# A delta-rule attention with two feed-forward layers on one core: the first block's state, Gram products and weight casts in another order

## The chip, the cores and the metric

One NeuronCore of a Trainium2 chip. The metric is the device time of one execution in microseconds (us); the number given for a kernel is the median of its runs.

## What is computed

Delta-rule attention over 32 heads (4 batches of 8) of 768 tokens and width 48: a state of 48 x 48 per head is read by the query and corrected by the key, token by token. Its output, 3072 tokens of width 384, goes through two feed-forward layers with hidden width 2048: the first with ELU, the second with h times sigmoid(1.702 h).

```python
for t in range(S):
    y[:, :, t] = einsum('bhd,bhde->bhe', q[:, :, t], state)
    v_old = einsum('bhde,bhd->bhe', state, kt)
    state = state + bt * einsum('bhd,bhe->bhde', kt, vt - v_old)
x = elu(x @ w_in) @ w_out          # layer 0
x = swish(x @ w_in2) @ w_out2      # layer 1
```

## The kernel before, in words

**Attention.** The tokens are cut into 12 chunks (c) of 64, two chunks to a pass (p, 0 to 5). In a chunk the token recurrence becomes a triangular system. Its parts are functions of `chunk`, `gram`, `inverse`, `join16` and `across`:

- `gram`: the products of the keys with themselves (L203), into the two-bank PSUM tile `wide` (there is one), copied to `z` by ScalarE in one whole copy (L190) and two for the far halves (`self.rest`, L193);
- `inverse`: for both chunks of a pass, rows of a 16 x 16 or 32 x 32 inverse on VectorE, two operations a row (L317, L322), then a scaling and a transpose (L330, L336). Passes 0 to 2 (`FINE`) have 16 x 16 blocks that `join16` (TensorE L395, L410) joins; `across` and, in pass 0, `t2`, `m1`, `m2` (L442, L457) give the off-diagonal part;
- `nv` scales v (VectorE, L490); `kq` is k times q (L504), `mask` masks it on VectorE (L515);
- `ks` is k times the state (L562), taken from v by VectorE (L567); `w` applies the inverse (L579, copies L585 to L588); `state` is the state's new part (L602), which VectorE adds to the old one (L609) or, for chunk 0, VectorE and ScalarE copy;
- `ya`, `yb`: the output (L629, L645), copied and split into high and low parts by ScalarE and VectorE (L655, L656).

`ks`, `kq`, `w`, `state`, the output and `m2` all use `wide` once the units run, so each waits until the one before it has been read.

**Units.** A unit is one block of 128 hidden columns (m, 0 to 15) for one pass's 512 tokens: 16 units for a pass, 6 passes, 2 layers, 192 units. Its nine up products (L748, high and low parts in fp32r) give `h`; ScalarE makes Relu and Exp (L757, L758), VectorE the second ELU step (L761), ScalarE the rounded hidden block `gh` (L770), VectorE the rest `gl` (L773). The nine down products (L785) come two units later (`LAG`) and sum in the three banks `acc0` to `acc2`; unit 2 is the first that does.

**Weights.** Layer 0's 16 weight blocks arrive as 64-bit words and are converted in pass 0's units by `prep`: `rebase` (ScalarE, L707), `shift` (VectorE, L714), `rest` (VectorE, L717, merges the words) with `high` (ScalarE, L724, the rounded part), and `low` (GpSimd, L728, the difference). Unit t does the shift, merge and cast of block t+2, the difference of block t+1, the rebase of block t+4, and the load of block t+6, which a one-element copy on ScalarE (L702) holds back. SP issues all loads, in program order.

**Order.** Everything is in one order written out by hand, and each engine takes its part of it in that order. First comes a straight list: both chunks of pass 0 up to their outputs, with the first weights and 11 steps of pass 1's inverse in between (`run(...)`, `also(n)`). Unit 0's up products start at 63.83 us. Then each unit emits: up products, first ELU step, `fill`, `gl` of the unit before, `mid`, second ELU step, down products of two units before, `end`, `gh`, `tail`. Attention of the passes to come is put at slots: slot s is the middle (even) or the end (odd) of unit s // 2. The steps of the inverses are spread over the `fill` of a range of units by `spread`, by costs in a table (`COST`, `slack`). Slots at issue here: Gram 4 at 0 and Gram 5 at 2, with their two extra copies in the tail of the same unit and the fill of the next; chunk 1's `state` at 4.

## Time and profile before

| | |
|---|---|
| median of 3 runs | 991.79 us (989.93 to 992.45) |
| profiled execution | 990.37 us |
| its span, first to last instruction | 988.6 us |
| TensorE busy | 941.7 us (95%) |
| VectorE, ScalarE, GpSimd busy | 594.4, 464.2, 83.1 us |
| mean granted TensorE clock | 0.984 of full |

In the rows PE is TensorE's matmuls and PEld its weight loads, DVE VectorE, ACT ScalarE, POOL GpSimd, SP the engine that issues the loads. A row names an operation as line, output tile <- input tiles. "idle before <- releaser" is the time that the engine stood idle ahead of it and whose end let it go; "issue" means that the profile shows nothing that it waited for. PEclk is the clock that TensorE was granted, as a share of 2.4 GHz. A busy TensorE at half clock does half the work.

### The profile page before, as it was taken

How to read it: one execution, taken by the hardware profiler on the slowest of the kernel's cores; microseconds unless marked ns; L12 is line 12 of the kernel's file. 1: busy time of each engine (PE TensorE's matmuls, PEld its weight loads, DVE VectorE, ACT ScalarE, POOL GpSimd, SP SyncE). 2: the span in 40 equal slices, each digit the busy share in tenths (PEclk: the TensorE clock that was granted, in tenths of full speed). 3: DMA queues.
4: the chain of work that ended last, by engine and by line, in shares of the span. 5: the costliest groups of instructions: out<-in, count | busy, mean ns of one | idle time of the engine just before them, and what ended most of it. 6: DMA issues, size and time to landing. Idle time of an engine off the chain costs nothing.

```text
span 988.6 us, 25639 instructions
## 1 busy us (share of the span) xinstructions
PE 941.7 (95%) x11520; PEld 773.2 (78%) x11520; DVE 594.4 (60%) x1048; ACT 464.2 (47%) x753; POOL 83.1 (8%) x72
## 2 busy tenths in 40 slices
PE   4866899999999999999999999999999999999998
PEld 4755677778878887888887888888888888888886
DVE  6886887677987877886445676733333333333332
ACT  6636475644374465444446675533333233333332
POOL 3021252010010001000000100101001001010000
PEclk9977999999999999999999999999999999999999
DMA  7263342303211230210114801010010010100000
GB/s 240 88 208 104 108 154 91 114 4 92 83 56 58 74 98 19 92 44 34 34 49 157 371 1 64 1 54 11 1 65 1 1 64 1 64 1 1 33 1 32
DMA packets 20174, 68.33 MB, mean 69 GB/s; under 512 B 3168, under 2 KB 4704, under 8 KB 20064
## 3 DMA queue, kind: packets, MB, share of 16 engines
q1 hardware_dynamic: 19920, 66.56, 20.0%
q8 instruction: 90, 1.47, 0.6%
q14 instruction: 20, 0.16, 0.1%
q10 hardware_dynamic: 144, 0.13, 0.0%
HBM read 57.25 MB, written 9.44 MB: 67 GB/s over the span
## 4 chain that ended last, share of the span: by engine, by line
PE 85%; DVE 8%; ACT 4%; issue 2%; DMA 0%; POOL 0%; ACTq 0%; DVEq 0%; POOLq 0%
PE h L748 38%; PE acc L785 27%; PE accn L785 10%; PE ps_w L562 1%; PE ps_w L504 1%; PE ps_w L579 1%; PE ps_w L602 1%; PE ps_w L629 1%; PE ps_w L203 1%; DVE tmp L317 1%; PE ps_w L645 1%; ACT z L193 1%; DVE t L761 1%; DVE W L322 1%; DVE x L515 1%
## 5 line engine op out<-in xcount | busy, mean ns | idle before, releaser
L748 PE MATMUL h<-xh,wt 128*128 128x512 f32 x1152 | 396.4, 398 | 0.0
L785 PE MATMUL acc<-gh,wt 128*128 128x512 f32 x864 | 292.6, 393 | 0.5 <-DVE xo L846 0.5
L748 PEld LDWEIGHTS h<-xh,wt 128*128 128x128 f32 x1152 | 218.5, 190 | 48.1 <-DVE xl L656 0.2
L748 PE MATMUL h<-xl,wt 128*128 128x512 f32 x576 | 226.6, 393 | 0.0
L773 DVE TENSOR_TENSOR gl<-t,gh 128x512 fp32r<-128x512 f32 x192 | 138.7, 722 | 93.8 <-ACT gh L770 93.6
L785 PEld LDWEIGHTS acc<-gh,wt 128*128 128x128 f32 x864 | 162.7, 188 | 35.7 <-issue 0.9
L770 ACT CAST gh<-t 128x512 fp32r<-128x512 f32 x192 | 119.3, 621 | 118.8 <-DVE t L761 62.2
L785 PE MATMUL acc<-gl,wt 128*128 128x512 f32 x432 | 168.7, 390 | 0.0
L767 DVE TENSOR_TENSOR t<-t,h 128x512 f32<-128x512 f32 x96 | 66.0, 687 | 168.9 <-ACT t L764 168.9
L764 ACT ACTIVATE t<-h 128x512 f32<-128x512 f32 x96 | 57.3, 597 | 187.2 <-PE h L748 187.2
L748 PEld LDWEIGHTS h<-xl,wt 128*128 128x128 f32 x576 | 109.5, 190 | 21.1
L757 ACT ACTIVATE t<-h 128x512 f32<-128x512 f32 x96 | 57.4, 598 | 100.3 <-PE h L748 99.8
L785 PE MATMUL accn<-gh,wt 128*128 128x512 f32 x288 | 96.4, 389 | 0.0
L761 DVE SCALAR_TENSOR_TENSOR t<-t,h 128x512 f32<-128x512 f32 x96 | 65.6, 684 | 51.0 <-ACT t L758 50.5
L785 PEld LDWEIGHTS acc<-gl,wt 128*128 128x128 f32 x432 | 81.4, 188 | 16.1
L785 PEld LDWEIGHTS accn<-gh,wt 128*128 128x128 f32 x288 | 54.1, 188 | 11.3
L758 ACT ACTIVATE t<-t 128x512 f32<-128x512 f32 x96 | 60.7, 632 | 3.1
L812 POOL TENSOR_TENSOR xl<-x1r,xh 128x512 fp32r<-128x512 f32 x18 | 24.1, 1339 | 407.4 <-ACT xh L811 314.4
L785 PE MATMUL accn<-gl,wt 128*128 128x512 f32 x144 | 56.0, 389 | 0.0
L728 POOL TENSOR_TENSOR wt<-w,wt 128x768 fp32r<-128x768 f32 x16 | 31.5, 1974 | 70.7 <-ACT wt L724 70.7
L515 DVE TENSOR_TENSOR x<-ps_w,mask_p 64x512 f32<-64x512 f32 x44 | 30.2, 687 | 11.2 <-PE ps_w L504 10.7
L717 DVE SCALAR_TENSOR_TENSOR w<-raw,w 128x768 uint32<-128x768 uint32 x32 | 35.2, 1101 | 0.9
(190 smaller groups left out, 832.6 us busy)
## 6 DMA issues: line engine op xcount, KB each, us to landing
raw<-in_w SPq DMA_DIRECT2D x32, 768.0 KB, 7.6
kt<-in_kT SPq DMA_DIRECT2D x12, 512.0 KB, 4.5
x<-in_qT SPq DMA_DIRECT2D x24, 256.0 KB, 4.2
kg<-in_kT SPq DMA_DIRECT2D x9, 512.0 KB, 4.8
kn<-in_kn SPq DMA_DIRECT2D x12, 384.0 KB, 3.5
x1d<-xo SPq DMA_DIRECT2D x12, 384.0 KB, 2.9
x1r<-x1d SPq DMA_DIRECT2D x6, 768.0 KB, 4.7
vn<-in_vn SPq DMA_DIRECT2D x11, 384.0 KB, 3.4
```

The lines of the kernel that those rows point to most:

```text
L515: v.tensor_tensor(out=g["x"][k][self.tok(k), 8 * hf:8 * hf + 8], in0=i, in1=self.mask_p[t].unsqueeze(1).to_broadcast(list(i.shape)), op=AL ...
L717: v.scalar_tensor_tensor(out=bits[m], in0=words(m, 0), scalar=29, in1=bits[m], op0=ALU.logical_shift_right, op1=ALU.bitwise_or)
L728: (v if layer else nc.gpsimd).tensor_tensor(out=wt[:, 1], in0=bits.pop(m).bitcast(F32), in1=wt[:, 0].bitcast(F32), op=ALU.subtract)
L748: nc.tensor.matmul(hps, wt[:, part, k * P:(k + 1) * P], src[:, k], start=(i == 0), stop=(i == 3 * NK - 1))
L757: nc.scalar.activation(out=t, in_=hps, func=AF.Relu, scale=-1.0)
L758: nc.scalar.activation(out=t, in_=t, func=AF.Exp, scale=-1.0)
L761: nc.vector.scalar_tensor_tensor(out=t, in0=t, scalar=-1.0, in1=hps, op0=ALU.add, op1=ALU.max)
L764: nc.scalar.activation(out=t, in_=hps, func=AF.Sigmoid, scale=1.702)
L767: nc.vector.tensor_tensor(out=t, in0=t, in1=hps, op=ALU.mult)
L770: nc.scalar.copy(gh, t)
L773: nc.vector.tensor_tensor(out=gl, in0=t, in1=gh.bitcast(F32), op=ALU.subtract)
L785: self.nc.tensor.matmul(self.acc[c], wt[:, part, DM + c * P:DM + (c + 1) * P], src, start=(m == 0 and i == 0), stop=(m == NM - 1 and i == 2),)
```

## The change

In the straight list: chunk 1's `nv` comes first, the first cast behind the rebase of block 2, the first difference ahead of chunk 0's output, and norm and scale of pass 1's inverse ahead of chunk 1's `w` (13 steps of that inverse instead of 11 before unit 0). Chunk 1's `state` goes to slot 0 and into `acc0`, `acc1`. Gram 4 and 5 go to slots 2 and 4, each with all three copies right behind it. In layer 0 the cast `high` leaves `rest` and stands first in the unit's `tail`, behind `gh`. Loads of chunk 2's k and chunk 3's v move by a unit, chunk 3's parts by half a unit to a unit and a half. Later passes: `m2` ahead of `ks`, and the last pass half a unit later. `spread` carries negative room over to the next unit.

```diff
--- before.py
+++ after.py
@@ -590,7 +590,7 @@
         def state():
             if last:
                 return
-            if first:
+            if c < 2:
                 ps = self.banks(0)
             else:
                 both = self.wide()
@@ -730,11 +730,12 @@
         ms = list(ms)
         steps = []
         for j, m in enumerate(ms):
-            t = [lambda m=m: shift(m), lambda m=m: (rest(m), high(m))]
+            t = [lambda m=m: shift(m), (lambda m=m: (rest(m), high(m))) if layer else (lambda m=m: rest(m))]
             if j:
                 t.append(lambda m=ms[j - 1]: low(m))
             steps += t
         steps.append(lambda: low(ms[-1]))
+        self.highs = [lambda m=m: high(m) for m in ms]
         return [lambda gate=False, m=m: load(m, gate) for m in ms], [lambda m=m: rebase(m) for m in ms], steps
 
     def up(self, wt, x, act_fn):
@@ -883,7 +884,11 @@
             sizes = sizes or [1.0] * len(fns)
             left = [max(0.2, 1.0 - taken.get(u, 0.0)) for u in range(u0, u1)]
             if u0 in slack:
-                left = [max(0.2, slack.get(u, 0.0) + (2.8 if u > NM - 3 else 1.2)) for u in range(u0, u1)]
+                left, over = [], 0.0
+                for u in range(u0, u1):
+                    over += slack.get(u, 0.0) + (2.8 if u > NM - 3 else 1.2)
+                    left.append(max(0.2, over))
+                    over -= left[-1]
             part, u, room = sum(left) / sum(sizes), u0, left[0]
             for f, size in zip(fns, sizes):
                 while room <= 0.0 and u + 1 < u1:
@@ -916,6 +921,7 @@
             return t.rearrange("p (u t) -> p u t", u=32)
 
         loads, bases, conv = self.prep(0, range(NM), lambda m: (self.wp, "wt"))
+        highs = self.highs
         join = {c: self.later(lambda c=c: self.join16(c, home), 6) for c in range(6)}
         part = {0: (0,), 1: (1, 2), 2: (3,), 3: (4, 5)}
         steps = self.later(lambda: self.inverse(0, lambda: turned(0)), len(self.sizes(0)))
@@ -983,17 +989,18 @@
         run(j1[4], j1[5], c1["t2"])
         also(2)
         run(bases[0], c0["m1"], c1["m1"], c0["nv"], c1["mask"], c0["m2"], bases[1], c1["m2"])
-        run(conv[0], conv[1], c0["ks"], c0["w"], c1["nv"], conv[2], bases[2], c0["state"])
+        run(c1["nv"], conv[0], c0["ks"], c0["w"], conv[1], bases[2], highs[0], c0["state"], conv[4])
         self.load_kn(1)
         for f in loads[4:6]:
             f()
-        run(c0["ya"], c1["ks"], conv[3])
+        run(conv[2], c0["ya"], c1["ks"], conv[3], highs[1])
         also(1)
         run(c0["yb"])
         also(2)
-        run(bases[3], c1["w"])
+        run(bases[3])
+        also(2)
+        run(c1["w"])
         nc.scalar.activation(out=self.one, in_=self.one, func=AF.Exp)
-        run(conv[4])
         also(6)
         run(c1["ya"], c1["yb"])
         self.early = False
@@ -1007,26 +1014,26 @@
 
         for m in range(2, NM):
             at(fill, m - 2, *conv[3 * m - 1:3 * m + 2])
-            at(tail, m - 2, *bases[m + 2:m + 3], *[lambda f=f: f(True) for f in loads[m + 4:m + 5]])
+            at(tail, m - 2, highs[m], *bases[m + 2:m + 3], *[lambda f=f: f(True) for f in loads[m + 4:m + 5]])
             taken[m - 2] = 0.37
         at(fill, NM - 2, conv[-1])
-        at(end, 2, lambda: self.load_kn(2))
-        for slot, c, i in ((4, 2, 0), (5, 2, 1), (7, 2, 3), (7, 3, 0), (8, 3, 1), (10, 3, 3)):
+        at(end, 1, lambda: self.load_kn(2))
+        for slot, c, i in ((4, 2, 0), (5, 2, 1), (7, 2, 3), (8, 3, 0), (8, 3, 1), (10, 3, 3)):
             at(end if slot % 2 else mid, slot // 2, *[join[c][k] for k in part[i]])
             use(slot, ("turned", "left", "", "right")[i])
         for slot, c, name in (
-            (4, 1, "state"), (6, 2, "kq"), (6, 2, "mask"), (8, 2, "nv"), (9, 3, "kq"), (9, 3, "mask"), (11, 2, "t2"),
-            (13, 2, "m1"), (12, 2, "ks"), (15, 2, "m2"), (16, 2, "w"), (18, 2, "state"), (18, 3, "nv"),
-            (20, 2, "ya"), (20, 2, "yb"), (21, 3, "ks"), (23, 3, "w"), (25, 3, "state"), (27, 3, "ya"), (27, 3, "yb"),
+            (0, 1, "state"), (6, 2, "kq"), (6, 2, "mask"), (7, 2, "nv"), (9, 3, "kq"), (9, 3, "mask"), (11, 2, "t2"),
+            (13, 2, "m1"), (12, 2, "ks"), (15, 2, "m2"), (16, 2, "w"), (18, 2, "state"), (21, 3, "nv"),
+            (20, 2, "ya"), (20, 2, "yb"), (22, 3, "ks"), (24, 3, "w"), (26, 3, "state"), (28, 3, "ya"), (28, 3, "yb"),
         ):
             u = slot // 2
             at(end if slot % 2 else mid, u, ch[c][name])
             use(slot, name)
-        for slot in (0, 2, 29, 32):
+        for slot in (2, 4, 30, 33):
             use(slot, "gram")
         if beside:
             spread(fill, 0, 3, [f for _, f in beside], [size for size, _ in beside])
-        at(end, 7, lambda: self.load_v(3))
+        at(end, 8, lambda: self.load_v(3))
         at(end, 9, lambda: self.load_kn(3))
         for slot, c, i in ((4, 4, 0), (4, 4, 1), (5, 4, 3), (6, 5, 0), (7, 5, 1), (9, 5, 3)):
             at(end if slot % 2 else mid, 16 + slot // 2, *[join[c][k] for k in part[i]])
@@ -1036,11 +1043,12 @@
             o = base[p - 1]
             a, b = 2 * p, 2 * p + 1
             first = (
-                (8, a, "kq"), (9, a, "t2"), (10, a, "m1"), (11, a, "ks"), (12, a, "m2"), (14, a, "w"),
+                (8, a, "kq"), (9, a, "t2"), (10, a, "m1"), (12, a, "ks"), (11, a, "m2"), (14, a, "w"),
             ) if p in self.FINE else (
-                (6, a, "t2"), (6, a, "kq"), (7, a, "m1"), (9 - (p in (3,)), a, "m2"), (8 + (p in (3,)), a, "ks"), (11, a, "w"),
+                (6, a, "t2"), (6, a, "kq"), (7, a, "m1"), (8, a, "m2"), (9, a, "ks"), (11, a, "w"),
             )
-            late = 2 if p in self.FINE else 0
+            late = 2 if p in self.FINE else int(p == NP - 1)
+            first = tuple((slot + (p == NP - 1), c, name) for slot, c, name in first)
             turn = (17, 15) if p in (3,5,) else (15, 17)
             for slot, c, name in first + (
                 (13 + late, a, "state"), (turn[0] + late, a, "ya"), (turn[0] + late, a, "yb"), (15 + late, b, "nv"),
@@ -1061,9 +1069,9 @@
         for p in range(2, NP):
             o = base[p - 1]
             if p == 2:
-                self.passes(at, spread, (mid, end, tail), fill, p, (0, 2), (6, o + 2), lambda: turned(2))
+                self.passes(at, spread, (mid, end, tail), fill, p, (2, 4), (6, o + 2), lambda: turned(2))
             else:
-                grams = (29, 32) if p == 3 else (2 * o - 32, 2 * o - 29)
+                grams = (30, 33) if p == 3 else (2 * o - 32, 2 * o - 29)
                 self.passes(at, spread, (mid, end, tail), fill, p, grams, (o - 11 if p == 3 else o - 13, o + 3))
 
 
@@ -1132,8 +1140,8 @@
 
         for slot, f in zip(grams, (first, lambda: self.gram(2 * p + 1, self.kg))):
             at(half[slot % 2], slot // 2, f)
-            at(half[2], slot // 2, lambda: self.rest[0]())
-            at(fill, slot // 2 + 1, lambda: self.rest[1]())
+            at(half[slot % 2 if p == 2 else 2], slot // 2, lambda: self.rest[0]())
+            at(half[slot % 2] if p == 2 else fill, slot // 2 + (p > 2), lambda: self.rest[1]())
         spread(fill, *steps, self.later(lambda: self.inverse(p, spare), n), self.sizes(p))
 
     def sizes(self, p):
```

## Rows read from the trace of the kernel before

**Rows 1.** Windows by stage: length, busy us of each engine, PEclk, DMA share, GB/s.
```profile
63.83:94.10 30.27, 19.47 (x357) 14.90 (x356) 22.00 (x42) 15.08 (x22) 5.80 (x3) 0.71 0.32 101
94.10:150.00 55.90, 50.41 (x1307) 40.08 (x1297) 43.60 (x70) 35.06 (x61) 19.70 (x12) 1.00 0.40 139
200.00:988.60 788.60, 782.02 (x7638) 640.70 (x7626) 444.48 (x755) 346.10 (x548) 35.55 (x29) 1.00 0.15 52
```

**Rows 2.** Waits of TensorE, 63 to 200 us: total, times, longest.
```profile
PE ps_w L203 <- ACT z L193: 7.7, 1, 7.7
PE ps_w L602 <- ACT z L193: 3.1, 1, 3.1
PE ps_w L562 <- DVE xl L656: 2.2, 1, 2.2
PE ps_w L504 <- issue: 1.6, 1, 1.6
```

**Rows 3.** Chain that ended last, 79 to 102 us: start, us, what.
```profile
79.12 1.99 PE ps_w L203 x64
...
81.11 4.10 PE h L748 x9
...
88.29 1.47 PE ps_w L602 x64
...
94.19 2.26 PE h L748 x9
...
101.01 2.26 PE h L748 x9
```

**Rows 4.** Waits of VectorE, 63.83 to 100 us: total, times, longest.
```profile
DVE su L609 <- PE ps_w L602: 5.8, 1, 5.8
...
DVE x L515 <- PE ps_w L504: 1.7, 1, 1.7
```

**Rows 5.** VectorE's groups, 63.8 to 94.1 us: busy us and mean ns, then idle before.
```profile
L317 DVE TENSOR_TENSOR tmp<-W 128x100 f32<-128x100 f32 (+6 forms) x10 | 4.0, 400 | 0.3
L717 DVE SCALAR_TENSOR_TENSOR w<-raw,w 128x768 uint32<-128x768 uint32 x4 | 3.8, 960 | 0.1
L714 DVE TENSOR_SCALAR w<-raw 128x768 uint32<-128x768 uint32 x4 | 3.2, 811 | 0.0
L322 DVE TENSOR_TENSOR W<-W,tmp 128x100 f32<-128x100 f32 (+6 forms) x10 | 2.5, 251 | 0.3
L609 DVE TENSOR_TENSOR su<-su,ps_w 48x384 f32<-48x384 f32 x4 | 2.2, 552 | 5.8 <-PE ps_w L602 5.8
```

**Rows 6.** Timeline around 70 us: start, us, engine, line.
```profile
70.14 1.88 POOL L728 TENSOR_TENSOR wt<-w,wt 128x768 fp32r<-128x768 f32 x1 [12.34 <-ACT wt L724]
...
70.36 1.75 DVE L317 TENSOR_TENSOR tmp<-W 128x72 f32<-128x72 f32 x1
```

**Rows 7.** Chain at unit 11: the nine up products behind the stall.
```profile
150.04 3.78 PE h L748 x9
```

**Rows 8.** Timeline of units 7 and 9; lines of weight difference, cast (min/median/max ns).
```profile
131.73 0.62 ACT L770 CAST gh<-t 128x512 fp32r<-128x512 f32 x1
...
135.06 0.39 PE L748 MATMUL h<-xh,wt 128*128 128x512 f32 x1
...
L728 POOL TENSOR_TENSOR wt<-w,wt x14: 1807/1872/2470, 70.1 to 167.0; 128x768 fp32r<-128x768 f32 x14
...
L724 ACT CAST wt<-w x14: 813/817/835, 69.2 to 166.0; 128x768 fp32r<-128x768 f32 x14
```

**Rows 9.** Waits of TensorE, 300 to 420 us.
```profile
PE ps_w L457 <- DVE vn L567: 1.3, 1, 1.3
```

**Rows 10.** Timeline of VectorE ahead of unit 0.
```profile
57.77 1.11 DVE L586 COPY su<-acc 64x384 f32<-64x384 f32 x2
...
58.92 0.18 DVE L286 TENSOR_SCALAR nb<-nb 128x32 f32<-128x32 f32 x1
...
60.86 0.21 DVE L301 STREAM_TRANSPOSE ntok<-nb 128x32 f32<-128x32 f32 x1
```

## The prediction

> **What bounds the kernel now.** I read the windows by stage first [rows 1]. From 200 us to the end TensorE is busy for 782.0 of 788.6 us at the full clock, so nearly all that can be won lies before. Units 0 to 2, from 63.83 to 94.10 us, are the poor stretch: TensorE works 19.5 of 30.3 us at a mean clock of 0.71. From 94.1 to 150 us it is busy for 50.4 of 55.9 us.
>
> Second come TensorE's waits [rows 2]. 7.7 us are Gram 5 waiting for ScalarE's copies of Gram 4, which share the one two-bank tile "wide"; 3.1 us are chunk 1's state product, again waiting for that tile; 2.2 us are the product of k with the state (ks) of chunk 3, waiting for the tile that chunk 2's output holds. The waits marked "issue" (the longest 1.6 us) have no releaser in the profile; I keep them as they are.
>
> Third is the chain in the same stretch [rows 3]: the late Gram 5 starts at 79.12, unit 2's nine up products follow at half clock (4.10 us against 2.26 at 94.19), and chunk 1's state comes only at 88.29.
>
> Last I asked whether something else would bind once those waits are gone. VectorE works 22.0 of the 30.3 us [rows 1], so it is the next bound. Its waits there [rows 4] are 5.8 us for chunk 1's state product and 1.7 us for chunk 2's k-q products; [rows 5] shows what its work is made of.
>
> **The change part by part.**
>
> *Chunk 1's state and the Grams.* The state product moves from the middle of unit 2 to the middle of unit 0 and into the banks of the down sums, which nothing uses until unit 2 sums for the first time. So it waits for neither Gram. Its four adds (2.2 us, [rows 5]) then run in unit 0, ahead of unit 0's second ELU step, where VectorE otherwise had rows of the inverse to do. Gram 4 and 5 move to units 1 and 2, each with its three copies directly behind it on ScalarE and no longer split over two units. Gram 5 still waits for Gram 4's copies, but a whole unit's products and the first down stand around it. On the SP queue the load of Gram 5's keys now stands behind a weight block's load, and chunk 2's k is loaded a unit earlier; the cover for the keys is that Gram 5 waits for Gram 4's copies anyway, and if it is too short the cost is a part of one block's transfer.
>
> *Two steps of pass 1's inverse go ahead of unit 0.* Ten steps are ten pairs, 4.0 + 2.5 us [rows 5], with 1.5 us of that a block [rows 6]: 0.5 us each, so 1.0 us leaves units 0 to 2.
>
> The gain of the stage goes by VectorE, as the bound. The wait of 5.8 us goes, since the state's product now stands right behind unit 0's up products. 1.0 us goes with the two steps. Of the 1.7 us for chunk 2's k-q products I take 1.2, since VectorE still has a weight block and one difference to do when they come. Together **-8.0 us**. Ends: -3.5, if VectorE is blocked once more in each of units 1 to 3 (3 x 1.5 us, [rows 6]), and -10.8, all of TensorE's idle time there (30.3 - 19.5, [rows 1]). I take the value nearer the upper end since VectorE's own wait rows add up to it.
>
> *The clock in this stretch.* TensorE will still pause in units 1 to 3: for unit 2's weights, for Gram 4's copies, for the last transpose of pass 1's inverse. I put the clock's change at 0. Ends: -1.8 (unit 2's nine at 2.26 instead of 4.10, [rows 3]) and +3.7 (two more up products at half clock).
>
> *The order ahead of unit 0.* Chunk 1's scaling of v, the first weights' cast and the state's copies change places, and norm and scale of the inverse (58.92 to 61.07, 2.1 us) now stand ahead of chunk 1's w copies (57.77), not behind them [rows 10]. But the weight difference on GpSimd that held VectorE there goes to an earlier place too. What comes before unit 0 is the same work in another order: 0, between -1 and +1.
>
> *Products half a unit later.* Chunk 3's v scaling, ks, w, state and output move by half a unit to a unit and a half. In unit 10 TensorE no longer meets ks right behind chunk 2's output: unit 11's up products come first (2.26 us), longer than the wait of 2.2 us [rows 2]. That stall goes, -2.2, and with it the fall of the clock behind it: the nine after it took 3.78 us, at full clock 2.26 [rows 7], -1.5. Together **-3.7**; ends -4.2 and, if the later ks meets the same late copies, -1.0.
>
> *Weight casts last on ScalarE.* In units 0 to 13 the cast (0.82 us, [rows 8]) moves from ahead of that unit's evacuations to behind its own cast of the hidden block. The evacuations gain up to 0.82 us; GpSimd's difference (1.87) starts later, and unit t+2 needs it. In the tightest place, unit 7, the hidden cast ends at 132.35 and unit 9 starts at 135.06: 2.71 us, against 0.82 + 1.87 = 2.69 [rows 8]. So it just fits, and a difference that takes 2.47 instead of 1.87 (its longest, [rows 8]) does not: 0.6, and some tenths elsewhere: **+0.7**; ends 0 and 21 (fourteen times 1.5, the third rival).
>
> One rule bears on this term. GpSimd's difference at 70.14 lasted 1.88 us, and VectorE's step that came 0.2 us later took 1.75 us where the other steps take about 0.25 [rows 5, 6]: the later of the two was held until the earlier ended. The Trainium skill, SBUF — State Buffer, section "Who interferes with whom", calls this an exclusive lock on the port pair the two share, taken by whichever starts first. By that rule it speaks against this change: the differences now start just when VectorE does the next block's shift and merge, so GpSimd could be the one that is held. By the row alone VectorE is the one held and the term stays at +0.7; by the rule in its other direction the term would be the third rival's.
>
> *Later blocks.* In block 4, ks no longer comes ahead of the second off-diagonal product, which waited 1.3 us for ks's tile [rows 9]: **-1.3**, between 0 and -1.3. The half-unit shift in the last block lies in the part where TensorE is busy throughout: 0. The carried-over room in the spreading of steps moves a few inverse steps of pass 2 from unit 13 to 14 and 15: 0, under TensorE's products.
>
> **Sum:** -8.0 - 3.7 + 0.7 - 1.3 = -12.3 us. The profiled execution took 990.37 us (span 988.6), 1.4 less than the median of the three runs; the sum gives 978.1 for it and 991.79 - 12.3 = **979.5 us** for the median.
>
> **The rivals.**
>
> *VectorE gives part of it back.* The differences block it once more in each of units 1 to 3: the stage yields 3.5, the stall at unit 10 yields 2.2 without the clock, block 4 1.3: -7.0, 984.8 us. For: VectorE at 22.0 of 30.3 us, and the block of 1.5 us seen. Against: that block was paid before as well.
>
> *TensorE's whole idle time comes back.* -10.8, unit 2 at full clock -1.8, -3.7 and -1.3: -17.6, 974.2 us. For: ScalarE has only 15.1 us of work there [rows 1]. Against: VectorE's work does not shrink.
>
> *The wait only changes its name.* The adds in unit 0 push back the second ELU step, the hidden cast, the weight cast and the difference in a row, so that unit 2 waits for its weights nearly as long as for Gram 5; the stage yields 1 and the later stalls are met by other late copies: about -2, 989.8 us. Against: VectorE's wait of 5.8 us would have to reappear elsewhere.
>
> *Slower: the difference is held behind shift and merge.* In each of fourteen units GpSimd waits out VectorE's two weight operations, (3.2 + 3.8) / 4 less blocks [rows 5], about 1.5 us, and TensorE's next unit but one waits as long: 14 x 1.5 = 21 - 12.3 = +8.7, 1000.5 us. It decides from 12.3 / 14 = 0.9 us per unit. For: the slack of 0.02 us in unit 7. Against: in [rows 6] GpSimd started amid VectorE's steps without delay. By the rule cited above either direction can occur.
>
> **How the numbers follow.** Forecast 0.52; VectorE 0.20; all idle time 0.12; name only 0.07; slower 0.09. The first three hold 0.84 and lie between about 974 and 985; with the bounds of the unknown terms the range is **974.0 to 987.5**. A measurement of this kernel can tell about 0.3%, 3 us, from no change. Faster by more: 0.52 + 0.20 + 0.12 = 0.84; within: 0.07; slower: 0.09.
>
> **What would show it.** Right: chunk 1's state product ahead of 72 us and no wait of it for the z copies; Gram 5's wait under 2 us; unit 4's up products near 93 us instead of 101.01 [rows 3]; VectorE without the 5.8 us wait; no 2.2 us wait ahead of chunk 3's ks, and unit 11's nine products at 2.26 us; block 4's 1.3 us gone. Wrong: waits of the up products for GpSimd's difference in many units, VectorE's shift and merge or the inverse's steps at 1.5 us and more in most units, or half clock beyond unit 4.

## The result and the profile after

The changed kernel takes **981.64 us** (979.57 to 984.06, 4 runs), the kernel before 990.93 (989.93 to 992.45, 4 runs): a ratio of 0.9906, 95% interval 0.9878 to 0.9934. Forecast were 979.5 us and a range of 974.0 to 987.5. The ratio is the time against that of the kernel before, run beside it. The profiled execution took 982.3 us, 8.1 less than the one of before, with a span of 980.6.

First the windows by stage, as in [rows 1]: units 0 to 2, units 3 to 10, and from 200 us to the end.

```profile
64.65:88.02 23.37, 17.16 (x358) 12.99 (x357) 19.92 (x38) 14.28 (x21) 3.71 (x2) 0.82 0.40 131
88.02:139.50 51.48, 49.46 (x1241) 38.91 (x1234) 45.40 (x65) 34.33 (x59) 18.97 (x12) 1.00 0.39 131
200.00:980.60 780.60, 774.88 (x7320) 634.58 (x7320) 441.39 (x750) 343.87 (x543) 35.49 (x29) 1.00 0.15 52
```

Units 0 to 2 take 23.4 us instead of 30.3, and VectorE is now busy for 19.9 of them, 85%. The prediction had it as the next bound; keys_first, below, asks after that. TensorE's waits from 55 to 200 us (columns as in [rows 2]):

```profile
PE acc L579 <- issue: 4.1, 1, 4.1
PE ps_w L203 <- DMA kg<-in_kT: 3.9, 1, 3.9
PE h L749 <- POOL wt L728: 2.5, 4, 1.2
PE h L645 <- issue: 2.4, 1, 2.4
PE ps_b L410 <- DVE w L384: 1.6, 1, 1.6
...
PE ps_w L504 <- issue: 1.1, 1, 1.1
PE h L749 <- ACT wt L724: 1.1, 1, 1.1
PE ps_w L203 <- ACT z L193: 0.8, 1, 0.8
```

Gram 5's 7.7 us for the copies of Gram 4, the state's 3.1 and the 2.2 of ks are gone. In their place stand 3.9 us of Gram 5 for its keys, 2.5 and 1.1 for weight blocks (difference and cast) and 1.6 for a transpose. The lines with "issue" are explained at the head of the experiments. The chain through units 0 to 3 (start, duration, what; compare [rows 3]):

```profile
67.73 0.88 PE acc L602 x64
...
73.89 0.33 SPq L703
...
74.75 0.02 SPq L151
...
74.80 5.84 DMA kg<-in_kT
80.64 0.14 issue
80.78 1.99 PE ps_w L203 x64
82.76 4.14 PE acc L786 x9
86.90 1.19 PE ps_b L395 x86
88.09 2.25 PE h L749 x9
```

Chunk 1's state comes at 67.73 instead of 88.29. But the load of Gram 5's keys (L151) is issued at 74.80, behind that of a weight block (L703), which ScalarE's chain holds back until 73.89; it lands 5.84 us later, and the first down products behind Gram 5 run at half clock (4.14 us; 0.51 of full granted from 82.69 to 86.90). So Gram 5 itself starts no earlier than before (80.78 against 79.12). What the change wins is the work that now stands ahead of it: the state's product and unit 2's up products, which begin at 73.04 instead of 81.11.

VectorE's waits from 64 to 95 us show the same from its side (compare [rows 4]):

```profile
DVE x L515 <- PE ps_w L504: 1.7, 1, 1.7
DVE su L609 <- PE acc L602: 1.1, 1, 1.1
```

The wait for the state's product is 1.1 us instead of 5.8; that for chunk 2's k-q products has stayed at 1.7.

The start of a unit, read from the timeline as its first up product, divides the whole difference; u4 is the start of unit 4 and so on, the figures are us:

| kernel | median of runs | start u0 | u0 to u4 | u4 to u7 | u7 to u16 | u16 to u22 | u22 to u191 |
|---|---|---|---|---|---|---|---|
| before | 990.93 | 63.8 | 37.1 | 23.1 | 53.9 | 36.6 | 761.9 |
| changed | 981.64 | 64.6 | 30.2 | 20.7 | 52.6 | 39.2 | 761.1 |
| state_alone | 988.24 | 64.2 | 33.5 | 22.8 | 55.4 | 37.0 | 762.1 |
| state_back | 988.17 | 64.0 | 34.1 | 21.1 | 52.5 | 40.5 | 760.9 |
| keys_first | 981.54 | 63.6 | 29.3 | 19.6 | 52.6 | 41.4 | 761.4 |
| cast_early | 983.12 | 63.0 | 28.0 | 22.7 | 50.0 | 39.0 | 760.4 |
| grams_back | 981.52 | 63.5 | 30.1 | 19.7 | 53.1 | 39.8 | 761.3 |
| chunk3_back | 985.12 | 64.4 | 29.8 | 19.5 | 54.1 | 41.4 | 760.8 |
| low_zero | 984.84 | 64.4 | 32.4 | 24.3 | 50.6 | 40.5 | 760.5 |
| three_parts | 978.45 | 63.5 | 27.7 | 22.7 | 50.0 | 40.0 | 760.6 |
| keys_grams | 980.57 | 65.2 | 29.9 | 19.2 | 53.2 | 38.7 | 761.1 |
| keys_grams_zero | 979.16 | 64.2 | 27.5 | 24.0 | 50.6 | 39.0 | 760.9 |
| later_back | 985.55 | 62.6 | 30.2 | 24.6 | 50.8 | 41.8 | 762.6 |
| list_back | 984.42 | 65.2 | 32.1 | 19.5 | 52.6 | 39.6 | 760.9 |

From before to changed: +0.8 (start of unit 0), -6.9, -2.4, -1.3, +2.6 and -0.9, together -8.0. The columns of the stages come from one profiled execution each, the medians from all runs; for cast_early the profiled one is the fastest (977.07), for low_zero nearly the slowest (986.59).

The kernel before was measured again beside each set of runs: its median was 990.93 beside the changed kernel and 992.88, 992.96 and 992.78 beside the others. A ratio goes against the before of its own set; a difference between medians of different sets is uncertain by about 2 us for that alone.

Nor is the column u0 to u4 free of scatter: unit 0's nine up products take 3.0 to 4.2 us in these fourteen profiles, by the clock that they meet. They took 4.2 in before (0.51 of full granted) and 3.1 in the changed kernel (0.73): 1.1 of the 6.9 us, which no run ties to an edit.

### The profile page after: what moved, and what is told of

Same layout as the page of the kernel before. It is cut to its first block, busy times and chain, and to the rows that moved or that the text cites. A ratio compares the mean times of both kernels' runs of the same rounds, so it can differ in the third digit from the quotient of the medians.

```text
span 980.6 us, 25655 instructions
## 1 busy us (share of the span) xinstructions
PE 939.2 (96%) x11520; PEld 769.4 (78%) x11520; DVE 601.4 (61%) x1048; ACT 463.8 (47%) x753; POOL 83.2 (8%) x72
## 4 chain that ended last, share of the span: by engine, by line
PE 82%; DVE 12%; ACT 3%; issue 2%; DMA 1%; SPq 0%; DVEq 0%; ACTq 0%
PE h L749 36%; PE acc L786 26%; PE accn L786 10%; PE ps_w L504 1%; DVE t L762 1%; DVE gl L774 1%; PE ps_w L562 1%; PE ps_w L579 1%; DVE w L717 1%; DVE W L322 1%; PE ps_w L629 1%; PE ps_w L203 1%; DVE tmp L317 1%; DVE su L609 1%; PE ps_w L645 1%
## 5 line engine op out<-in xcount | busy, mean ns | idle before, releaser
L749 PEld LDWEIGHTS h<-xh,wt 128*128 128x128 f32 x1152 | 216.1, 188 | 52.5 <-POOL wt L728 4.9
L774 DVE TENSOR_TENSOR gl<-t,gh 128x512 fp32r<-128x512 f32 x192 | 141.7, 738 | 88.8 <-ACT gh L771 88.6
L786 PEld LDWEIGHTS accn<-gh,wt 128*128 128x128 f32 x288 | 54.1, 188 | 11.2
L717 DVE SCALAR_TENSOR_TENSOR w<-raw,w 128x768 uint32<-128x768 uint32 x32 | 36.8, 1149 | 0.9
L515 DVE TENSOR_TENSOR x<-ps_w,mask_p 64x512 f32<-64x512 f32 x44 | 30.3, 688 | 8.7 <-PE ps_w L504 8.2
```

What stands on the lines that cost most here:

```text
L515: v.tensor_tensor(out=g["x"][k][self.tok(k), 8 * hf:8 * hf + 8], in0=i, in1=self.mask_p[t].unsqueeze(1).to_broadcast(list(i.shape)), op=AL ...
L717: v.scalar_tensor_tensor(out=bits[m], in0=words(m, 0), scalar=29, in1=bits[m], op0=ALU.logical_shift_right, op1=ALU.bitwise_or)
L749: nc.tensor.matmul(hps, wt[:, part, k * P:(k + 1) * P], src[:, k], start=(i == 0), stop=(i == 3 * NK - 1))
L774: nc.vector.tensor_tensor(out=gl, in0=t, in1=gh.bitcast(F32), op=ALU.subtract)
L786: self.nc.tensor.matmul(self.acc[c], wt[:, part, DM + c * P:DM + (c + 1) * P], src, start=(m == 0 and i == 0), stop=(m == NM - 1 and i == 2),)
```

## The experiments

The stretch from u4 to u7 has to be read first, since it runs through all of them.

**A pause that no edit explains.** TensorE's instructions stand in the same order up to unit 13 in changed, grams_back and later_back. Yet u4 to u7 takes 20.7, 19.7 and 24.6 us. What differs is a pause without a releaser inside one group, the 64 products of chunk 3's k and q. In the timeline of the changed kernel (start, duration, instruction, idle before):

```profile
100.65 0.44 PE L504 MATMUL ps_w<-x,kt 48*64 48x64 f32 x11
102.19 1.03 PE L504 MATMUL ps_w<-x,kt 48*64 48x64 f32 x53 [1.10 <-issue]
103.16 0.50 PE L749 MATMUL h<-xh,wt 128*128 128x512 f32 x1
```

And of low_zero (below), whose pause falls behind the same eleventh product:

```profile
102.74 0.44 PE L504 MATMUL ps_w<-x,kt 48*64 48x64 f32 x11
105.11 1.03 PE L504 MATMUL ps_w<-x,kt 48*64 48x64 f32 x53 [1.93 <-issue]
106.07 0.67 PE L752 MATMUL h<-xh,wt 128*128 128x512 f32 x1
106.54 0.63 PE L752 MATMUL h<-xl,wt 128*128 128x512 f32 x1
```

Behind the pause of 1.10 a product runs in 0.50 and less (full clock; 1.00 granted), behind that of 1.93 in 0.63: half clock (0.56 granted up to 109.97). later_back has 1.9 here and 1.0 at L442 (unit 6), grams_back 0.2 and none. So this stretch spreads over 5 us between kernels that are the same there, and a profile's verdict on an edit is read from the other columns.

What TensorE waits for in these pauses is its next instructions. The page of the changed kernel lists, among the DMA queues (packets, MB, share of 16 engines):

```profile
q8 instruction: 90, 1.47, 0.6%
```

Each of these packets moves 16 KB, and the records behind the traces give their times. In the changed kernel one runs from 99.98 to 100.94, and the pause ends at 102.19, 1.25 us after it; in low_zero one runs from 102.94 to 103.90, and the pause ends at 105.11, 1.20 after it. Over the fourteen traces TensorE has 71 idle times of more than 0.2 us that are marked "issue", and all 71 end 1.20 to 1.57 us behind the end of such a packet; of its 232 idle times with a releaser, 7 do. The lines of L579 and L645 ahead of unit 0 belong to the 71. In the kernels without a pause in this group, or with one of 0.2, the packet starts 2.1 to 2.6 us ahead of the group; in the others it starts from 0.7 ahead of it to 0.2 behind its start. Why it starts when it does, no run shows.

**state_alone**: the kernel before with chunk 1's state moved, nothing else.

```diff
-            if first:
+            if c < 2:
...
-            u = slot // 2
+            u = 0 if (c, name) == (1, "state") else slot // 2
```

Expected: 

> The kernel before, with one part of the change: chunk 1's state product in the middle of unit 0 and in the banks of the sums. My theory (VectorE's wait for the state is most of the gain, but Gram 5 must also be free of Gram 4's copies): Gram 5 still waits for the copy of Gram 4 that stands in unit 1, and the state's adds (2.2 us) now stand ahead of unit 0's second ELU step, so Gram 5 comes no earlier than 79.1 us. What is saved is the state's own wait (3.1 us) and its product: unit 4 starts 3 to 4 us earlier, and the time is 2 to 4 us less than before. Rival (the state's move alone makes the gain): 7 to 9 us less than before.

Measured: 988.24 us, ratio 0.9945 (0.9927 to 0.9964). Units 0 to 3 give 3.6 us, as my theory had it (the medians give 4.6), and Gram 5 now waits longer than before:

```profile
PE ps_w L203 <- ACT z L193: 10.2, 1, 10.2
```

**state_back**: the changed kernel with the state where it was (middle of unit 2, in "wide").

```diff
-            if c < 2:
+            if first:
...
-            u = slot // 2
+            u = 2 if (c, name) == (1, "state") else slot // 2
```

Expected: 

> The changed kernel with chunk 1's state back in the middle of unit 2, in the wide tile, ahead of Gram 5; the Grams stay in units 1 and 2. My theory: Gram 5 then waits for the state's four adds on VectorE, which come behind unit 1's rest of the hidden block, so Gram 5 starts near 86 us instead of 80.8 and unit 4 4 to 6 us later than in the changed kernel: 985 to 987 us. Rival (the Grams' move makes the gain): within 1.5 us of the changed kernel.

Measured: 988.17, ratio 0.9943 (0.9920 to 0.9965), 1.2 us over my theory's range. Unit 4 starts 3.9 us later, counted from unit 0, and Gram 5 waits for the adds of the state:

```profile
PE ps_w L203 <- DVE su L609: 7.9, 1, 7.9
```

So each move clears one holder of "wide", and Gram 5's wait passes to the next holder, 10.2 and 7.9 us long. The gain does come in parts all the same: against before, u0 to u4 is 3.6 us shorter with the state's move alone, 3.0 with the rest of the change without it, and 6.9 with both. The two nearly add up. The rest of the change includes the steps that list_back asks after.

**keys_first**: Gram 5's keys loaded ahead of weight block 6.

```diff
-            at(tail, m - 2, highs[m], *bases[m + 2:m + 3], *[lambda f=f: f(True) for f in loads[m + 4:m + 5]])
+            at(tail, m - 2, highs[m], *bases[m + 2:m + 3], *[lambda f=f: f(True) for f in loads[m + 4:m + 5] if m > 2])
...
-        at(end, 1, lambda: self.load_kn(2))
+        at(end, 1, lambda: self.load_kn(2), lambda: loads[6](True))
```

Expected: 

> The changed kernel with the load of Gram 5's keys ahead of weight block 6 on SP's queue (the weight block's load moves to the end of unit 1). My theory (the 3.9 us wait of Gram 5 for its keys is on the path, by way of the half clock of the first down products): the wait falls below 1 us, Gram 5 starts near 78 us, unit 3 starts at 85 to 86 us instead of 88.0, and the time is 2 to 3 us less than the changed kernel's. Rival (VectorE alone sets the pace there): unit 4 starts within 0.7 us of 94.8 and the time is the same within 1 us.

Measured: 981.54, ratio 0.9878 (0.9848 to 0.9908): no different from the changed kernel. The keys' load is issued at 71.72, its wait is gone, and u0 to u4 gains 0.8 of 3.9 us (unit 0's nine up products took 0.8 more than in the changed kernel). Behind it the last transpose of pass 1's inverse is late, and Gram 5 waits for ScalarE's copies:

```profile
PE ps_b L395 <- DVE xl L336: 1.9, 1, 1.9
...
PE ps_w L203 <- ACT z L193: 1.1, 1, 1.1
```

So the keys' wait mostly covered these two, VectorE's above all, and 2.2 us more are lost from u16 to u22, in a part that this edit does not touch.

**low_zero** takes away what holds VectorE: GpSimd writes zeros as the low part of layer 0's weights instead of the difference, so those low parts are left out.

```diff
-            (v if layer else nc.gpsimd).tensor_tensor(out=wt[:, 1], in0=bits.pop(m).bitcast(F32), in1=wt[:, 0].bitcast(F32), op=ALU.subtract)
+            if layer:
+                v.tensor_tensor(out=wt[:, 1], in0=bits.pop(m).bitcast(F32), in1=wt[:, 0].bitcast(F32), op=ALU.subtract)
+            else:
+                nc.gpsimd.memset(wt[:, 1].bitcast(F32), 0.0)
```

Expected: 

> The changed kernel with GpSimd writing zeros in place of the weights' difference in layer 0, so layer 0 lacks the low parts of its weights. VectorE's steps that are held by GpSimd's difference add up to about 14 us in units 0 to 14 of the changed kernel, 8 us in the kernel before. My theory (VectorE sets the pace in units 1 to 3 and 13 to 16, so these blocks cost part of the gain): the steps of 1.4 us and more vanish, TensorE no longer waits for the difference, and the time is 3 to 6 us less than the changed kernel's. Rival (VectorE has slack enough to hide the blocks): within 1.5 us of the changed kernel.

Measured: 984.84, ratio 0.9918 (0.9898 to 0.9939), not faster. The merges (L717) from 64 to 165 us, in the changed kernel and then in low_zero (count, busy us, mean ns, idle before):

```profile
L717 DVE SCALAR_TENSOR_TENSOR w<-raw,w 128x768 uint32<-128x768 uint32 x14 | 16.5, 1176 | 0.5
```

```profile
L717 DVE SCALAR_TENSOR_TENSOR w<-raw,w 128x768 uint32<-128x768 uint32 x14 | 13.4, 959 | 0.5
```

The held steps vanish with the difference: 1176 ns become 959. The Trainium skill, SBUF — State Buffer, section "Who interferes with whom", says that a VectorE instruction with two inputs in SBUF contends with a GpSimd instruction that reads SBUF, but not with one that only writes it; these two rows agree. The time did not follow: in this execution Gram 5 waited 6.1 us for its keys, u4 to u7 took 3.6 us more with the long pause at L504, and only u7 to u16 gained, 2.0. My theory fell as it was put; what the held steps cost had to be asked with the keys' wait gone (keys_grams_zero).

**cast_early**: the weights' cast back in the unit's fill.

```diff
-            at(fill, m - 2, *conv[3 * m - 1:3 * m + 2])
-            at(tail, m - 2, highs[m], *bases[m + 2:m + 3], *[lambda f=f: f(True) for f in loads[m + 4:m + 5]])
+            at(fill, m - 2, *conv[3 * m - 1:3 * m + 1], highs[m], *conv[3 * m + 1:3 * m + 2])
+            at(tail, m - 2, *bases[m + 2:m + 3], *[lambda f=f: f(True) for f in loads[m + 4:m + 5]])
```

Expected: 

> The changed kernel with the weight cast back in its old place, behind the merge of the words and ahead of the unit's evacuations. My theory (the cast's late place costs TensorE its waits for GpSimd's difference, 2.5 us in four places, and 1.1 us for the cast, but most of them lie ahead of a wait that ends later anyway): these waits go, the time is between 1 us more and 2 us less than the changed kernel's. Rival (the late cast is a large part of the gain, since it frees the evacuations): 3 us or more slower than the changed kernel.

Measured: 983.12, ratio 0.9895 (0.9866 to 0.9924); of eight runs two took 977.1 and 977.4, six 982.2 to 984.3, and the profile is of the fastest. There, no wait for a difference or a cast is left between 63 and 163 us, u0 to u4 is 2.1 and u7 to u16 2.6 shorter, though Gram 5 waited 5.5 us for its keys. By the medians the edit shows nothing; 983.12 is 0.5 us above my theory's range.

**chunk3_back**: chunk 3's scaling, ks, w, state and output in their old slots.

```diff
-            (13, 2, "m1"), (12, 2, "ks"), (15, 2, "m2"), (16, 2, "w"), (18, 2, "state"), (21, 3, "nv"),
-            (20, 2, "ya"), (20, 2, "yb"), (22, 3, "ks"), (24, 3, "w"), (26, 3, "state"), (28, 3, "ya"), (28, 3, "yb"),
+            (13, 2, "m1"), (12, 2, "ks"), (15, 2, "m2"), (16, 2, "w"), (18, 2, "state"), (18, 3, "nv"),
+            (20, 2, "ya"), (20, 2, "yb"), (21, 3, "ks"), (23, 3, "w"), (25, 3, "state"), (27, 3, "ya"), (27, 3, "yb"),
...
-            use(slot, name)
+            use(dict(nv=21, ks=22, w=24, state=26, ya=28, yb=28).get(name, slot) if c == 3 else slot, name)
```

The last line keeps the spreading of the inverse's steps as the changed kernel has it.

Expected: 

> The changed kernel with chunk 3's v scaling, ks, w, state and output at their old slots. My theory (the later ks removes a stall of 2.2 us and a fall of the clock of 1.5 us): ks of chunk 3 waits again 1.5 to 2.5 us for chunk 2's output, and the time is 2 to 4 us more than the changed kernel's. Rival (the copies in front of it come earlier now, so the stall would be gone anyway): wait below 0.7 us, time within 1 us.

Measured: 985.12, ratio 0.9926 (0.9908 to 0.9945), 3.5 us over the changed kernel's median, though the two intervals overlap. The wait of ks is back, and a Gram waits longer than in the changed kernel (0.8):

```profile
PE ps_w L203 <- ACT z L193: 2.5, 1, 2.5
PE ps_w L562 <- DVE xl L656: 2.4, 1, 2.4
```

The fall of the clock did not come back with it: unit 11's nine up products took 2.33 us, against 3.78 in before. In the profile u7 to u16 is 1.5 us longer and u16 to u22 2.2, where the Gram waits. So the stall of the prediction is shown, and its price of 1.5 us for the clock is not, by this run.

**grams_back**: pass 3's Grams half a unit earlier, as before the change.

```diff
-                grams = (30, 33) if p == 3 else (2 * o - 32, 2 * o - 29)
+                grams = (29, 32) if p == 3 else (2 * o - 32, 2 * o - 29)
```

The reason lies in the changed kernel's timeline of VectorE:

```profile
174.41 2.10 DVE L336 STREAM_TRANSPOSE kg<-W 128x1024 f32<-128x1024 f32 x1 [3.67 <-PE ps_w L203]
...
183.21 0.69 DVE L774 TENSOR_TENSOR gl<-t,gh 128x512 fp32r<-128x512 f32 x1 [0.96 <-ACT gh L771]
185.48 0.71 DVE L384 STREAM_TRANSPOSE w<-kg 128x512 f32<-128x512 f32 x1 [1.58 <-DMA x1d<-xo]
```

and of TensorE:

```profile
173.18 1.16 PE L203 MATMUL ps_w<-kg 48*64 48x64 f32 x64 [0.84 <-ACT z L193]
...
186.34 1.25 PE L410 MATMUL ps_b<-w 16*32 16x16 f32 x128 [1.64 <-DVE w L384]
```

The last transpose of pass 2's inverse writes the tile "kg" that Gram 7 reads. Gram 7, half a unit later, holds it back 3.67 us; behind it stand the next rest, the second ELU step and the copies of the first output, whose transfer the step at 185.48 waits for, and TensorE waits for that.

Expected: 

> The changed kernel with pass 3's Grams at their old slots (Gram 6 at the end of unit 14, Gram 7 in the middle of unit 16). My theory (in the changed kernel the last transpose of pass 2's inverse waits 3.7 us on VectorE for Gram 7, because it writes the tile that Gram 7 reads, and this hands back about 2 us of the gain in units 16 to 19): that wait falls below 1 us, unit 20 starts 1.5 to 2.5 us earlier counted from unit 0, and the time is 1 to 2.5 us less than the changed kernel's. Rival (the inverse's rows crowded into units 14 to 16 make the loss): the wait goes, unit 20 starts less than 0.5 us earlier.

Measured: 981.52, ratio 0.9888 (0.9869 to 0.9907), the time of the changed kernel. The transpose waits 1.20, and u16 to u19 falls from 19.4 to 17.6. It is lost again at once, in the chain of waits:

```profile
181.48 0.69 PE ps_b L410 x56
182.17 1.18 issue
183.35 0.68 PE ps_b L410 x52
184.03 3.83 PE h L749 x9
```

A pause of 1.18 us inside the join's 128 products, and the nine up products behind it at half clock (0.56 granted), 3.83 us against 2.26 at 187.58 in the changed kernel. There, with TensorE waiting for VectorE at the same place, no such pause shows. It is one of the 71: in grams_back the instruction packet runs from 180.98 to 181.92 and the pause ends 1.43 us later; in the changed kernel it runs from 182.64 to 183.58, well ahead of the join's start at 186.34, so the wait for VectorE covered it.

**three_parts**: keys_first, grams_back and cast_early together.

Expected: 

> The changed kernel with three parts altered at once: Gram 5's keys loaded ahead of weight block 6, pass 3's Grams at their old slots, the weight cast back in its old place. My theory (three losses in three places, which add up): about 2 us for each, 975 to 978 us, unit 20 at least 4.5 us earlier counted from unit 0 than in the changed kernel. Rival (what one part gains, the next wait takes): 979.5 us or more.

Measured: **978.45** (974.04 to 979.07, 5 runs), ratio 0.9845 (0.9823 to 0.9868): faster than both kernels, the interval below the changed kernel's (0.9878 to 0.9934). It lies 0.5 us above my theory's range; unit 20 starts 3.3 us earlier counted from unit 0, not 4.5. From unit 0 to unit 4 one wait is left, Gram 5 for the copies of Gram 4 (3.7).

**keys_grams**: the same without cast_early.

Expected: 

> Gram 5's keys loaded ahead of weight block 6, and pass 3's Grams half a slot earlier, at 29 and 32, with the cast last as in the changed kernel. My theory: the keys' gain reaches unit 18 (keys_first showed it) and is lost there to the last transpose of pass 2's inverse, which waits for Gram 7; with the Grams earlier it is kept, so the time comes to 977.5 to 979.5, as the kernel with all three edits has it, and the cast's place is worth under 1 us. Rival: the cast carried that kernel, and without it this one takes 981 to 982 with waits for GpSimd's difference in units 10 to 14.

Measured: 980.57, ratio 0.9885 (0.9865 to 0.9905), a microsecond over my theory's upper end, and with the waits for GpSimd's difference that the rival named (first line):

```profile
PE h L749 <- POOL wt L728: 2.4, 4, 1.2
...
PE ps_b L395 <- DVE xl L336: 1.9, 1, 1.9
...
PE h L749 <- ACT wt L724: 1.1, 1, 1.1
```

Against three_parts it is 2.2 us longer from u0 to u4 and 3.2 from u7 to u16. The rival is the nearer: the cast's old place carries more of that kernel than I held, though the two intervals still touch.

**keys_grams_zero**: the same with the difference replaced by zeros, as in low_zero.

Expected: 

> The kernel above, but the weights' low parts of layer 0 are written as zeros by GpSimd instead of computed as a difference (so layer 0 leaves out its low weight products' values; their products still run). If the steps of VectorE that GpSimd's difference holds (some 14 us in units 0 to 14 of the changed kernel) still cost TensorE something once the keys' wait is gone: 1.5 to 3 us less than the kernel above. Rival: VectorE's held steps lie beside TensorE's work, and the two agree within 1 us.

Measured: 979.16, ratio 0.9867 (0.9846 to 0.9888): 1.4 under keys_grams, between the two expectations. Stage by stage it is plainer: u0 to u4 2.4 shorter, u7 to u16 2.6, and u4 to u7 4.9 longer by the pause (1.7) and a second one of 0.75 in unit 5, with 0.64 of the clock granted behind that one (105.15 to 108.40). So the difference does cost TensorE time, by two ways that these runs do not separate: it holds VectorE, and it is itself late.

**later_back**: the two edits of the later blocks undone.

```diff
-                (8, a, "kq"), (9, a, "t2"), (10, a, "m1"), (12, a, "ks"), (11, a, "m2"), (14, a, "w"),
+                (8, a, "kq"), (9, a, "t2"), (10, a, "m1"), (11, a, "ks"), (12, a, "m2"), (14, a, "w"),
...
-                (6, a, "t2"), (6, a, "kq"), (7, a, "m1"), (8, a, "m2"), (9, a, "ks"), (11, a, "w"),
+                (6, a, "t2"), (6, a, "kq"), (7, a, "m1"), (9 - (p in (3,)), a, "m2"), (8 + (p in (3,)), a, "ks"), (11, a, "w"),
...
-            late = 2 if p in self.FINE else int(p == NP - 1)
-            first = tuple((slot + (p == NP - 1), c, name) for slot, c, name in first)
+            late = 2 if p in self.FINE else 0
```

Expected: 

> The changed kernel with the second off-diagonal product ahead of ks again in the later blocks, and the last block half a unit earlier, as before. My theory: block 4's wait of 1.3 us comes back and the last block's end gains some tenths; 0 to 1.5 us slower than the changed kernel, too little to tell apart. Rival: the gain in these blocks is the same with both orders, within 0.3 us in the profile from 200 us to the end.

Measured: 985.55, ratio 0.9928 (0.9911 to 0.9946). Block 4's wait is back:

```profile
PE ps_w L457 <- DVE vn L567: 1.3, 1, 1.3
```

From u22 to u191 it takes 1.5 us more than the changed kernel (from u40 to u80 0.9, which is also what the change gained there against before). Within that, units 50 to 59 lose 1.4 and 60 to 71 lose 0.7, and units 72 to 79 win 1.2: there the last block's shift by half a unit had cost something. The rest of the 3.9 us lies in parts that the edit does not touch, u4 to u7 (the pause) and unit 19 (8.2 us at a mean clock of 0.65, 5.5 in the changed kernel).

**list_back**: the straight list ahead of unit 0 in its old order, 11 steps of the inverse.

```diff
-        run(c1["nv"], conv[0], c0["ks"], c0["w"], conv[1], bases[2], highs[0], c0["state"], conv[4])
+        run(conv[0], conv[1], highs[0], c0["ks"], c0["w"], c1["nv"], conv[2], bases[2], c0["state"])
...
-        run(conv[2], c0["ya"], c1["ks"], conv[3], highs[1])
+        run(c0["ya"], c1["ks"], conv[3], highs[1])
...
-        run(bases[3])
-        also(2)
-        run(c1["w"])
+        run(bases[3], c1["w"])
...
+        run(conv[4])
```

Expected: 

> The changed kernel with the straight list ahead of unit 0 in the order of before (11 steps of pass 1's inverse ahead of unit 0, chunk 1's scaling of v in its old place). My theory: unit 0 starts within 1 us of the changed kernel and VectorE has two more steps in units 0 to 2, 1.0 us, most of it hidden; the time is 0 to 1.5 us more. Rival: the two steps are worth more than their time, because VectorE is the bound there: unit 4 starts 2 us or more later after unit 0, and the time is 3 us more.

Measured: 984.42, ratio 0.9932 (0.9906 to 0.9957). Unit 0 starts 0.6 us later, u0 to u4 takes 1.9 more (0.7 of it in unit 0's nine up products), and the join at the end of unit 2 waits 1.5 us for VectorE's last transpose (L336). That is the rival's place and nearly its size; the intervals overlap with the changed kernel's, so it is likely and not shown.

## Why the prediction was right, and where it was not

The sum was -12.3 us, the profile shows -8.0; sign and range held, the 981.64 us lie 2.1 over the forecast. Part of that is luck: 2.4 of the 8.0 us came from u4 to u7, where nothing had been forecast. Without them the profile would show -5.6, less than half of the sum.

Of the signs of being right two failed: Gram 5 waited 3.9 us, not under 2, and unit 4 began at 94.8, not near 93. The other signs came, and none of those of being wrong: four waits for a difference are not many units, VectorE's long steps beside it are in about half of the units, and no up or down products ran at half clock beyond unit 4.

- **State and Grams, two steps ahead of unit 0** (-8.0): -6.9, of which 1.1 is unit 0's clock. The mechanism is shown from both sides: state_alone and state_back each give about half, with Gram 5 waiting 10.2 and 7.9 us. Of the terms inside, VectorE's wait for the state fell by 4.7 of 5.8 us, and the 1.2 us for chunk 2's k-q products did not come: that wait is 1.7 as before, and it stands behind this stretch. The step that failed is the cover for the keys, "a part of one block's transfer": their load was put behind a weight block's and was issued 5.6 us later than before (74.80 against 69.19), which cost Gram 5 3.9 us. Yet taking that wait away gave 0.8: VectorE came next (1.9). So the first rival, VectorE giving part back, was right about what binds there and wrong about the size.
- **The clock** (0): unit 2's up products do run at full clock, but the half clock moved to the first down products (4.14, where before had 4.10 and 3.24 in the two groups). The net is about -0.9, inside the range given.
- **The list ahead of unit 0** (0): +0.8 in the profile, by the waits for instructions at L579 and L645 (4.1 and 2.4; in the same view of the kernel before 2.7 and 1.2); unit 0 starts between 62.6 and 65.2 in the fourteen kernels. The prediction had left such waits out ("I keep them as they are").
- **Products half a unit later** (-3.7): right in the mechanism. Neither the stall nor the half clock behind it is left in the changed kernel, and unit 11's nine up products run at full clock. But u7 to u16 is only 1.3 us shorter than before, because the late casts of the next point took the rest there: with the cast early (cast_early, three_parts) it is 3.9 shorter. What the clock's fall alone was worth stays open, since chunk3_back brought back the stall without it.
- **Casts last on ScalarE** (+0.7): mis-sized. I added up one tight place, unit 7, and took the others as "some tenths". TensorE waited 2.5 us in four places for differences and 1.1 for a cast; with the cast early these waits are gone, and u0 to u4 and u7 to u16 are 2.1 and 2.6 shorter. The price in the time of all runs stays open: -1.5 by the medians of cast_early, +2.1 by those of three_parts and keys_grams. The slower rival (the last of the list; the text calls it the third) did not come: no difference took over 2.56 us.
- **Pass 3's Grams** were not in my sum at all. They moved by half a slot, which I passed over, and through "kg" they cost u16 to u19 2.0 us in the profile; the time of all runs does not show it, since the wait for instructions took the place (grams_back). This is the miss of kind: a moved product was followed to who reads its output, but not to who writes over its input.
- **Later blocks** (-1.3): -0.9. Block 4 gives 1.4, as forecast; the last block's shift, put at 0, costs about half a microsecond.
- u4 to u7 gained 2.4 us that I had not forecast, most of it by shorter waits for instructions; this is not the change's merit by any run.

## What to carry to other kernels

Where several products share one tile, look for all its holders: when one is freed, the wait passes to the next, and here each gave about half of what both gave. When a step is moved, ask three times: who reads what it writes, who overwrites what it reads, and which loads now queue ahead of its own. And before a microsecond in a profile is given to an edit, look at the same stretch in kernels that do not differ there; a pause marked "issue" should be held against the times of the instruction packets.

## What was unexpected in the hardware

TensorE runs out of instructions. In the middle of a group of small products, behind the eleventh or twelfth of 64, it stood still for 0 to 1.9 us from kernel to kernel, and ahead of unit 0 for up to 5.2 us (keys_grams, L579). All 71 such pauses end 1.20 to 1.57 us after a 16 KB instruction packet has been moved. A stall that is taken away can therefore uncover such a wait some instructions later, as in grams_back and three_parts. What sets the start of a packet stays open.

The length of a pause does not by itself settle the clock behind it: in unit 4 the pauses of 1.1 to 1.8 us were followed by nine up products at full clock (2.33 to 2.37 us in seven kernels), the two of 1.93 by 0.56 and 0.67 granted, but the one of 1.18 in grams_back's join by 0.56 too.
